# Turning first rows in single PSUM banks, long-filter rows by whole blocks, and the last hT turn later

## Chip, cores and metric

The kernel runs on one core of a Trainium2 chip. The metric is the device time of one execution in microseconds (us); smaller is better. TensorE is written PE in the profile, VectorE DVE, ScalarE ACT, GpSimd POOL and SyncE SP.

## The reference

A block of a network, forward and backward in one launch, in bf16, for 2048 rows of 1024 channels:

```python
xn = layernorm(A_q)                                  # rows of 1024
k_shift = 4-tap causal convolution of A_k along the rows
kv = k_shift * A_v
y = irfft(rfft(kv, 4096) * rfft(A_ssm_k, 4096))[:2048]   # long convolution, per channel
s = xn * (y + kv * A_ssm_D)
h = (xn @ B_w_gate) * (xn @ B_w_up)                  # 1024 -> 3584
out = A_q + s * silu(h @ B_w_down)                   # 3584 -> 1024
```

Returned are `out` and the gradients of all ten inputs but `B_x` for a given `grad_out`.

## The kernel before

A row tile is 128 rows; there are 16, numbered b. The work runs in stages, and PE carries matrix products in all of them:

- **Head, 0 to about 70 us.** `layer_norm` normalizes row tiles in chunks of 1, 1, 2, 4, 4 and 4 (`chunks`, `xs`): statistics on DVE (L584, L585), a root on ACT (L592), the normalizing itself on DVE (L603). Each tile is then turned (transposed) on PE in blocks of 128x128 into PSUM and copied by ACT into `XNT`, the stationary side of the products. Tiles 0 and 1 are turned in two halves of four blocks (L609, copied at L610), tiles 2 to 7 in one bank of eight (L620, copied at L621), and tiles 8 to 15 by `turn_late` (L571, copied at L631).
- **Gate and up products, 9 to about 505 us.** `gu_unit(sl, b0, n, ...)` multiplies n row tiles with a slab of 256 columns of both weights (L673, eight products of 512 columns for a row tile into one bank `psg` of `ps_gu`, which has two), copies to `gut` on ACT (L675) and stores it. A unit's element-wise product `hN` (called h, not the long filter) runs on DVE one unit later (`hn[0]`), and is turned to `hT` by `turn` or `turn_pair` through `defer` and `flush`, then stored from SP.
- **Forward long convolution, beside those products.** The generator `conv_forward` gives DVE work piece by piece. It is pumped by `tick`, which is called once for each row tile of a unit and lets the generator run up to a share of `F_TOTAL`; the yields are weights in us, less 0.95 of `pe_us`, an account of the PE work that it adds. Its PE parts are transforms (L234, L239, into `ps_cv`), inverse transforms (L455) and the turn of the long filter, `h_rows(ds)`, once for each of 8 groups of 128 channels: `hrow[:, c, u, r]` holds a filter's 2048 taps of a channel in a partition, and a block takes every eighth tap, so the columns of the stationary operand lie 8 elements apart. The result, scaled on ACT (L791), is `hx`.
- **Down product, 505 to 711 us**, `bm_first` and `late_mm` (L1032), in pairs of row tiles and 28 steps `fc`; a step of `bm_first` is a pair of products for each of two row tiles. After its first four steps `flush()` turns the last `hN`. Then the pools `ps_gu`, `fg` and `fw` go, and `ub` takes their room, into which the last weights `WD` and the next `ht` rows are loaded from SP.
- **Backward**, 700 us to the end.

Two forms of turning are in use. The plain one multiplies a block of 128 rows by the identity. `turn_halves` splits it into rows 0 to 63 and 64 to 127: two matmuls of 64 rows and 64 columns, with a result bank for each half; ACT's copy puts the halves together (`halves`).

PSUM has 8 banks. In the head `ps_tr` holds one tile `tr` of two banks (`tr_tile`, shared by `turn`, `turn_pair` and `h_rows`), `ps_gu` two banks, and `ps_st` one tile `turns` of four banks, out of which `next_bank` deals; after the head `ps_st` goes and `ps_cv` takes the four banks. Waits between engines are set by the framework from tiles, pools and the order of the program, which a scheduler rearranges; `tc.issue_after` and `keep_in_program_order` pin some of it.

Of the kernel before, what the change touches and what calls it, by code (L numbers as in the profile page):

```python
# [13 lines left out]
BF16 = mybir.dt.bfloat16  # L14
# [5 lines left out]
def build_kernel(  # L20
# [66 lines left out]
    def pool(name, bufs=1, side=None, space=None):  # L87
        kw = dict(name=name, bufs=bufs, reuse_waits="tile")
        if side:
            kw["side"] = side  # L90
        if space is not None:
            kw["space"] = space
        return tc.alloc_tile_pool(**kw)
# [425 lines left out]
    fg = pool("fg", 2, side="right")  # L519
    ps_tr = pool("ps_tr", 1, space=PSUM)  # L520
    ps_gu = pool("ps_gu", 2, space=PSUM)
    ps_st = pool("ps_st", 1, space=PSUM)
    turns = ps_st.tile([P, 4, 2, 4, P], BF16, name="tr")
    bank = [0]

    def next_bank():
        bank[0] += 1
        return turns[:, bank[0] % 4]

    busy = turns[:, 0].rearrange("p a b x -> p (a b x)").bitcast(F32).rearrange("p (a x) -> p a x", a=4)  # L530

    def keep_busy(n):
        for i in range(n):
# [40 lines left out]
    def halves(x):  # L574
        return x.rearrange("p b (h u) -> p h b u", h=2)

    def layer_norm(b0, n, x4):
        def small(name, dt=F32):
            return lns.tile([P, 4], dt, name=name)[:, 0:n]
        mv = lns.tile([P, 4, 2], F32, name="mv")[:, 0:n, :]  # L580
        for i in range(n):
            bst = lns.tile([P, 2, 6], F32, name="bst")
            for hh in range(2):
                V.bn_stats(out=bst[:, hh, :], in_=x4[:, i, hh * 512:(hh + 1) * 512])  # L584
            V.bn_aggr(out=mv[:, i, :], in_=bst[:])  # L585
        var_b = small("var_b", BF16)
        V.tensor_copy(var_b, mv[:, :, 1])
        vpe = small("vpe", BF16)
        V.tensor_scalar(vpe, var_b, EPS, None, op0=ADD)
        half_r = small("half_r")  # L590
        with tc.issue_after(act_copy[0].ins) if act_copy[0] is not None else nullcontext():
            root = nc.scalar.activation(half_r, vpe, ACT.Sqrt, scale=0.25)  # L592
        q0 = small("q0")
        rec = small("rec")
        V.reciprocal(rec, half_r)
        tt(q0, vpe, rec, MUL)
        sq_b = small("sq_b", BF16)
        V.scalar_tensor_tensor(sq_b, q0, 0.25, half_r, op0=MUL, op1=ADD)
        V.reciprocal(RSTD[:, b0:b0 + n], sq_b)
        for i in range(n):  # L600
            b = b0 + i
            q, qi = divmod(b, 4)
            last = V.tensor_scalar(x4[:, i, :], x4[:, i, :], mv[:, i, 0:1], RSTD[:, b:b + 1], op0=SUB, op1=MUL)  # L603
            if b < 2:
                for hh in range(2):
                    ps = next_bank()[:, 0]
                    for dc in range(4):
                        d0 = (4 * hh + dc) * P
                        tr_ln[0] = nc.tensor.transpose(ps[:, dc, :], x4[:, i, d0:d0 + P], ident[:])  # L609
                    act_copy[0] = nc.scalar.copy(out=XNT[0][:, 4 * hh:4 * hh + 4, b * P:b * P + P], in_=ps)  # L610
                if b == 0:
                    with tc.issue_after(tr_ln[0].ins):
                        keep_busy(10)
                continue
            if b0 >= 8:
                turn_rows.append((x4[:, i, :], q, qi))
                continue
            ps = next_bank().rearrange("p a b x -> p (a b) x")
            for dc in range(DC):
                tr_ln[0] = nc.tensor.transpose(ps[:, dc, :], x4[:, i, dc * P:(dc + 1) * P], ident[:])  # L620
            act_copy[0] = nc.scalar.copy(out=XNT[q][:, :, qi * P:(qi + 1) * P], in_=ps)  # L621
        c, r0 = divmod(b0, 8)
        return last, root, st(xnn[:, c, r0:r0 + n, :], x4[:, 0:n, :])

    def turn_late():
        ps = turns[:].rearrange("p (h j) i b x -> p h j i (b x)", h=2).rearrange("p h j i (a u) -> p h (j i) a u", u=64)
        for i, (x, q, qi) in enumerate(turn_rows):
            for dc in range(DC):
                tr_ln[0] = turn_halves(lambda hh: ps[:, hh, i, dc], x[:, dc * P:(dc + 1) * P])
        for i, (x, q, qi) in enumerate(turn_rows):  # L630
            act_copy[0] = nc.scalar.copy(out=halves(XNT[q][:, :, qi * P:(qi + 1) * P]), in_=ps[:, :, i])  # L631
        turn_rows.clear()

    nop = lambda: None
# [4 lines left out]
    def tr_tile():  # L639
        return ps_tr.tile([P, 2, 8, P], BF16, name="tr")  # L640
# [101 lines left out]
    def conv_forward():  # L742
# [33 lines left out]
            st(KSHd[dp], U[6][:].rearrange("p (b d) -> p b d", b=NB))  # L776
            yield 2.3

        def h_rows(ds):
            if ds == 8:  # L780
                return
            hrow = S_["h", ds]
            hx = S_["hx"] = cf.tile([P, NB, P], BF16, name="hx")
            pe_us[0] += 0.67
            ps = tr_tile()[:].rearrange("p h b x -> p h (b x)").rearrange("p h (b u) -> p h b u", u=64)
            with tc.issue_after(tr_ln[0].ins):
                turn_halves(lambda hh: ps[:, hh, 0], hrow[:, 0, :, 0])
            for b in range(1, 16):
                turn_halves(lambda hh: ps[:, hh, b], hrow[:, b // 8, :, b % 8])
            for c in range(2):  # L790
                nc.scalar.activation(halves(hx[:, 8 * c:8 * c + 8, :]), ps[:, :, 8 * c:8 * c + 8], ACT.Copy, scale=WSC)  # L791
            h_out.append(ds)
            if ds + 1 < 8:
                load_h(ds + 1)

        def kvs(ds):
            return S_["kvt", ds // 2][:, :, ds % 2 * P:(ds % 2 + 1) * P]
# [62 lines left out]
        yield from shift(0)  # L860
        PIN[0] = True
        yield 3.9
        h_rows(0)
        yield 0.1
        tl = turn_tables(ps_cv)
        sp = [half(0, S_["hx"], i, Dz[:, 0:P]) for i in range(2)]
        for ds in range(8):
            yield 0.5
            if ds % 2 == 1 and ds < 7:
                with tc.issue_after(S_["kst"].ins):  # L870
                    for c in range(2):
                        load_kv(ds // 2 + 1, c)
            D0 = Dz[:, ds * P:(ds + 1) * P]
            sph = []
            KX = cx.tile([P, 16, 256], BF16, name="KX")
            HX = cs.tile([P, 16, 256], BF16, name="HX", bufs=2)
            own_room = lambda X: X[:].rearrange("p a x -> p (a x)").bitcast(F32).rearrange("p (a x) -> p a x", a=8)[:, 0:4]
            eight = (ds, 1) in EIGHT
            if ds == 0:
                yield from transform(0, 1, sp, HX, own_room(KX), lambda i: sph.append(half(0, kvs(0), i)), nop)  # L880
            else:
                yield from transform(ds, 0, sp, KX, own_room(HX), lambda i: sph.append(half(ds, S_["hx"], i, D0)), nop)
                S_["kst"] = st(KFd[ds], KX[:])
            calls = []

            def behind():
                calls.append(0)
                if len(calls) % 2 == 0:
                    next(tl, None)
            room = cf.tile([P, 4, 256], F32, name="room", tag="hx")[:] if eight else None  # L890
            yield from transform(ds, int(ds > 0), sph, HX if ds else KX, room, nop1 if eight else lambda c: h_rows(ds + 1) if c == 0 else None,
                                 behind)
            if ds == 0:
                S_["kst"] = st(KFd[0], KX[:])
            if eight:
                h_rows(ds + 1)
            turned(HX, 1, 0, 1)
            yield 1.3
            if ds == 7:
                cf.release()  # L900
                S_["filters"] = False
            st(HFd[ds], HX[:])
            yield from product(KX, HX, KX, cs, False, 0)
            if ds % 2 == 1 and ds < 7:
                yield from shift(ds // 2 + 1)
            sp = []

            def ahead():
                if ds < 7:
                    sp.append(half(ds + 1, kvs(ds + 1), len(sp)))  # L910
            yield from (inv8 if ds in INV8 else inv_dft)(KX, HX, cs, ahead if ds % 2 == 0 else None, ahead)
            if ds % 2 == 1:
                ahead()
            S_["G", ds] = HX
            tl = tail(ds)
# [4 lines left out]
        cx.release()  # L920
        kst.release()

    F_TOTAL = 4 * SHIFT_W + 3.0 + 8 * (0.5 + FWD4_W + 1.3 + PROD_W + INV_W) + 10.0 - 0.95 * 8 * (4 * 1.75 + 0.67 + 4 * 0.9)
    F_TOTAL += len(EIGHT) * (FWD8_W - 9.6 + 0.95 * 1.75) - 2.0
    F_TOTAL += len(INV8) * (INV8_W - INV_W + 0.95 * 1.8)
    conv = conv_forward()
# [46 lines left out]
    st(RSTN[:], RSd.rearrange("(b p) -> p b", p=P))  # L973
    for p_ in (lnp, lns, tg, bsb):
        p_.release()
    ps_st.release()
    ps_cv = pool("ps_cv", 2, space=PSUM)
    pump, drain, step = make_pump(conv, F_TOTAL)
    cnt = [-5]
# [66 lines left out]
    cv_gone.append(True)  # L1046
    ps_bm = pool("ps_bm", 2, side="right", space=PSUM)
    pss = [ps_bm.tile([P, D], F32, name="psbm") for i in range(2)]
    with tc.issue_after(bm_first(range(4)).ins):
        flush()  # L1050
    for p_ in (ps_gu, fg, fw):
        p_.release()
# [11 lines left out]

    with tc.issue_after(wd_ld.ins):
        ht1 = load_ht1()
    fc_ = 4
    while conv_state["filters"]:
        bm_first([fc_])
        fc_ += 1  # L1070
# [735 lines left out]
```

## Time and profile before

| | us |
|---|---|
| median of 3 runs | 1915.76 (1915.6 to 1915.89) |
| profiled execution | 1915.97 |
| its span in the profile | 1914.2 |
| PE busy | 1895.2 (99%) |
| DVE busy | 1550.7 (81%) |
| ACT busy | 637.1 (33%) |

A line of the timeline gives the start in us, the length of the merged stretch, the engine, the source line, the operation, what it writes and reads, the shape, how many instructions are merged, and in brackets the idle time of the engine in front of it with what ended it. PEld is the loading of a stationary operand, which runs beside PE. Matmuls are pipelined: an instruction's own length is longer than the distance to the next start, so the time of a group is read from its start to the start of what follows.

### The profile page before, as it was taken

The numbers are of one execution on the slowest core, as the hardware profiler recorded it, in microseconds if no ns is written. First come the engines' busy times: TensorE is split into PE (matmuls) and PEld (weight loads), VectorE is DVE, ScalarE is ACT, GpSimd is POOL, SyncE is SP. The second block draws the span as 40 slices with busy tenths as digits, with TensorE's granted clock in tenths as the row PEclk, the third lists the DMA queues.
The fourth block names the chain that finished last, engine by engine and source line by source line (L and its number), as shares of the span: only waits on it lengthen the run. The fifth ranks groups of instructions, "written<-read, shape, count | busy, mean of one in ns | idle before, by whom it ended". The sixth has DMA issues, their size and how long they took to land.

```text
span 1914.2 us, 28265 instructions
## 1 busy us (share of the span) xinstructions
PE 1895.2 (99%) x11367; PEld 1014.8 (53%) x11507; DVE 1550.7 (81%) x1711; ACT 637.1 (33%) x927; POOL 334.8 (17%) x465
## 2 busy tenths in 40 slices
PE   8999999999999999999999999999999999999999
PEld 4555555545444456666666665664444444444444
DVE  7999999999988556887999999999995205678862
ACT  5765555546433233432222222222222102011122
POOL 5121212111113220001031221111212101112120
PEclk9999999999999999999999999999999999999999
DMA  8777866769769997677888698585887999889963
GB/s 285 269 251 232 257 224 207 234 233 296 248 228 311 313 306 230 208 239 229 275 264 264 221 266 267 181 286 177 227 245 173 221 203 180 182 176 195 194 162 124
DMA packets 425107, 444.35 MB, mean 232 GB/s; under 512 B 268400, under 2 KB 342796, under 8 KB 410512
## 3 DMA queue, kind: packets, MB, share of 16 engines
q1 hardware_dynamic: 367504, 239.03, 46.7%
q0 software_dynamic: 41152, 174.15, 29.3%
q10 hardware_dynamic: 16320, 29.36, 4.1%
q8 instruction: 90, 1.47, 0.3%
q14 instruction: 41, 0.34, 0.1%
HBM read 193.87 MB, written 189.84 MB: 200 GB/s over the span
## 4 chain that ended last, share of the span: by engine, by line
PE 96%; DVE 1%; issue 1%; ACT 1%; DMA 1%; SPq 0%; ACTq 0%; DVEq 0%
PE psb L1497 20%; PE psx L1642 20%; PE psg L673 19%; PE psb L1480 10%; PE psb L1580 9%; PE psbm L1032 9%; PE psF L234 3%; PE tr L571 1%; PE psI L455 1%; PE psY L1191 1%; PE psY L445 1%; PE psx L1580 1%; DMA U<-in_A_q_dram 1%; ACT U L631 0%; DVE bst L584 0%
## 5 line engine op out<-in xcount | busy, mean ns | idle before, releaser
L673 PE MATMUL psg<-wslab,U 128*128 128x512 bf16 x1728 | 399.0, 380 | 5.2 <-ACT gut L675 1.2
L1497 PE MATMUL psb<-U,U 128*128 128x512 bf16 x1792 | 397.1, 379 | 0.0
L1642 PE MATMUL psx<-U,dgut 128*128 128x512 bf16 x1505 | 331.0, 379 | 1.6
L1642 PEld LDWEIGHTS <-dgut 128*128 128x128 bf16 x1792 | 175.3, 98 | 211.4
L1497 PEld LDWEIGHTS <-U 128*128 128x128 bf16 x1792 | 175.2, 98 | 198.0
L673 PEld LDWEIGHTS <-U 128*128 128x128 bf16 x1792 | 172.4, 98 | 195.0 <-issue 3.5
L1480 PE MATMUL psb<-wdt,U 128*128 128x256 bf16 x1792 | 205.6, 273 | 0.0
L1480 PEld LDWEIGHTS <-U 128*128 128x128 bf16 x1792 | 175.3, 98 | 29.2
L212 DVE TENSOR_TENSOR W<-W 128x1024 f32<-128x1024 f32 (+1 forms) x189 | 186.5, 1003 | 4.1
L1580 PE MATMUL psb<-U,U 128*128 128x512 bf16 x797 | 176.1, 379 | 0.9
L1502 ACT CAST wb<-psb 128x512 bf16<-128x512 f32 x112 | 65.6, 586 | 315.4 <-PE psb L1497 313.4
L1247 DVE SCALAR_TENSOR_TENSOR dkp<-dkT,kT 128x1024 bf16<-128x1024 bf16 (+2 forms) x64 | 78.3, 1224 | 97.7 <-DMA dkT<-DKSHd 96.0
L1032 PE MATMUL psbm<-U,ht 128*128 128x512 bf16 x658 | 145.0, 379 | 0.7
L1580 PEld LDWEIGHTS <-U 128*128 128x128 bf16 x896 | 87.4, 98 | 104.3
L675 ACT CAST gut<-psg 128x512 bf16<-128x512 f32 x156 | 91.6, 589 | 117.0 <-PE psg L673 108.9
L1674 ACT ACTIVATE dx_t<-dxn 128x1024 bf16<-128x1024 f32 x15 | 15.9, 1057 | 323.1 <-DVE dxn L212 317.7
L1032 PEld LDWEIGHTS <-ht 128*128 128x128 bf16 x672 | 65.6, 98 | 78.2
L212 DVE TENSOR_TENSOR U<-U,dht 128x2048 bf16<-128x2048 bf16 x56 | 68.3, 1221 | 46.8 <-ACT dht L1482 46.7
L1482 ACT CAST dht<-psb 128x512 bf16<-128x512 f32 x112 | 65.6, 587 | 116.3 <-PE psb L1480 116.3
L66 POOL DMA_DIRECT2D Hd<-hN x54 | 37.3, 690 | 261.2 <-DVE hN L212 259.0
L1621 ACT CAST wbs<-psb 128x512 bf16<-128x512 f32 x51 | 29.9, 586 | 145.4 <-PE psb L1580 134.4
L212 DVE TENSOR_TENSOR W<-SP 128x1024 f32<-128x1024 f32 x64 | 74.2, 1218 | 1.6 <-ACT SP L295 1.1
(259 smaller groups left out, 2342.2 us busy)
## 6 DMA issues: line engine op xcount, KB each, us to landing
U<-GUd SPq DMA_DIRECT2D x28, 1024.0 KB, 8.9
DGd<-U SPq DMA_DIRECT2D x28, 1024.0 KB, 6.2
GUd<-gut ACTq DMA_DIRECT2D x39, 512.0 KB, 5.8
out_dram<-wb SPq DMA_DIRECT2D x112, 128.0 KB, 4.9
U<-Hd SPq DMA_DIRECT2D x14, 1024.0 KB, 6.7
Hd<-hN POOLq DMA_DIRECT2D x54, 256.0 KB, 5.0
HTd<-hT SPq DMA_DIRECT2D x24, 512.0 KB, 4.1
ht<-HTd SPq DMA_DIRECT2D x18, 512.0 KB, 7.6
```

Of the source, the lines that this page charges most:

```text
L212: pinned(V.tensor_tensor(o, a, b, op))
L234: mm = nc.tensor.matmul(ps[:, k].rearrange("p (c d) -> p c d", c=2), T[:, r, k, :], xr[:, r], start=(n == 0), stop=(n == len(rs) - 1 and ( ...
L673: gu_mm[0] = nc.tensor.matmul(ps[:], XNT[q][:, dc, qi * P:(qi + 1) * P], w[:, dc].rearrange("p a f -> p (a f)"), start=(dc == 0), stop=(dc ...
L675: nc.scalar.copy(out=gut[:, :, i], in_=ps[:].rearrange("p (a f) -> p a f", a=2))
L1032: mm = nc.tensor.matmul(ps[:, dh * 512:(dh + 1) * 512], ht(fc)[:, i * P:(i + 1) * P], WD[fc // 4][:, fc % 4, dh * 512:(dh + 1) * 512], sta ...
L1247: ins = V.scalar_tensor_tensor(prod[:].rearrange("p r d -> p (r d)")[:, lo:H], dkT[:, 0, lo:H], 1.0, kT[:, 0, 13 + m + lo:13 + m + H], op0 ...
L1480: nc.tensor.matmul(ps[:, x * SLW:(x + 1) * SLW], DBMT[2 * hf + g][:, dc, (b % 4) * P:(b % 4 + 1) * P], wdt[:, dc, :], start=(dc == 0), sto ...
L1482: nc.scalar.copy(out=dht[:, 2 * e:2 * e + 2].rearrange("p b f -> p (b f)"), in_=ps[:])
L1497: nc.tensor.matmul(ps[:], XN[b // 4][:, b % 4, dc * P:(dc + 1) * P], dgus[b // 8][:, :, b % 8], start=(b == 0), stop=(b == NB - 1))
L1502: nc.scalar.copy(out=wb[:, dc % 2].rearrange("p a f -> p (a f)"), in_=ps[:])
L1580: nc.tensor.matmul(ps, h[:, f, b, :], DBM[b // 4][:, b % 4, dh * 512:(dh + 1) * 512], start=(b == 0), stop=(b == NB - 1))
L1642: nc.tensor.matmul(ps[:, dh * 512:(dh + 1) * 512], t[n][:, f, i * P:(i + 1) * P], WGU[n][:, f, dh * 512:(dh + 1) * 512], start=(n == 0 and ...
```

## The change

- `ps_st` becomes a pool of four tiles of one bank each. `busy` and every turn of row tiles 0 to 7 take a tile of their own.
- In `turn_late` that pool is released and a pool of two tiles of two banks follows in the same four banks. Two row tiles are turned into one tile and copied, then the next two.
- `h_rows` turns the long filter plainly, in blocks of 128x128, in two calls of eight blocks (c = 0 and 1) into one bank each, with one ACT copy each. The calls stand where `transform` calls `ahead(0)` and `ahead(1)`, two pieces of DVE work apart (or before and after `turned` where the eight-point form is used). The weights in `pe_us` and `F_TOTAL` follow.
- The last `flush()` of `hT` comes after eight steps of `bm_first` in place of four.

The built program has 128 matmuls and 128 weight loads fewer on PE, and the same number of instructions on the other engines.

```diff
@@ -519,15 +519,9 @@
     fg = pool("fg", 2, side="right")
     ps_tr = pool("ps_tr", 1, space=PSUM)
     ps_gu = pool("ps_gu", 2, space=PSUM)
-    ps_st = pool("ps_st", 1, space=PSUM)
-    turns = ps_st.tile([P, 4, 2, 4, P], BF16, name="tr")
-    bank = [0]
-
-    def next_bank():
-        bank[0] += 1
-        return turns[:, bank[0] % 4]
-
-    busy = turns[:, 0].rearrange("p a b x -> p (a b x)").bitcast(F32).rearrange("p (a x) -> p a x", a=4)
+    ps_st = [pool("ps_st", 4, space=PSUM)]
+
+    busy = ps_st[0].tile([P, 4, P], F32, name="tr")
 
     def keep_busy(n):
         for i in range(n):
@@ -603,11 +597,11 @@
             last = V.tensor_scalar(x4[:, i, :], x4[:, i, :], mv[:, i, 0:1], RSTD[:, b:b + 1], op0=SUB, op1=MUL)
             if b < 2:
                 for hh in range(2):
-                    ps = next_bank()[:, 0]
+                    ps = ps_st[0].tile([P, 4, P], BF16, name="tr")
                     for dc in range(4):
                         d0 = (4 * hh + dc) * P
                         tr_ln[0] = nc.tensor.transpose(ps[:, dc, :], x4[:, i, d0:d0 + P], ident[:])
-                    act_copy[0] = nc.scalar.copy(out=XNT[0][:, 4 * hh:4 * hh + 4, b * P:b * P + P], in_=ps)
+                    act_copy[0] = nc.scalar.copy(out=XNT[0][:, 4 * hh:4 * hh + 4, b * P:b * P + P], in_=ps[:])
                 if b == 0:
                     with tc.issue_after(tr_ln[0].ins):
                         keep_busy(10)
@@ -615,20 +609,24 @@
             if b0 >= 8:
                 turn_rows.append((x4[:, i, :], q, qi))
                 continue
-            ps = next_bank().rearrange("p a b x -> p (a b) x")
+            ps = ps_st[0].tile([P, DC, P], BF16, name="tr")
             for dc in range(DC):
                 tr_ln[0] = nc.tensor.transpose(ps[:, dc, :], x4[:, i, dc * P:(dc + 1) * P], ident[:])
-            act_copy[0] = nc.scalar.copy(out=XNT[q][:, :, qi * P:(qi + 1) * P], in_=ps)
+            act_copy[0] = nc.scalar.copy(out=XNT[q][:, :, qi * P:(qi + 1) * P], in_=ps[:])
         c, r0 = divmod(b0, 8)
         return last, root, st(xnn[:, c, r0:r0 + n, :], x4[:, 0:n, :])
 
     def turn_late():
-        ps = turns[:].rearrange("p (h j) i b x -> p h j i (b x)", h=2).rearrange("p h j i (a u) -> p h (j i) a u", u=64)
-        for i, (x, q, qi) in enumerate(turn_rows):
-            for dc in range(DC):
-                tr_ln[0] = turn_halves(lambda hh: ps[:, hh, i, dc], x[:, dc * P:(dc + 1) * P])
-        for i, (x, q, qi) in enumerate(turn_rows):
-            act_copy[0] = nc.scalar.copy(out=halves(XNT[q][:, :, qi * P:(qi + 1) * P]), in_=ps[:, :, i])
+        if turn_rows and len(ps_st) == 1:
+            ps_st[0].release()
+            ps_st.append(pool("ps_s2", 2, space=PSUM))
+        for i in range(0, len(turn_rows), 2):
+            ps = ps_st[1].tile([P, 2, 2, DC, 64], BF16, name="tr2")
+            for j, (x, q, qi) in enumerate(turn_rows[i:i + 2]):
+                for dc in range(DC):
+                    tr_ln[0] = turn_halves(lambda hh: ps[:, hh, j, dc], x[:, dc * P:(dc + 1) * P])
+            for j, (x, q, qi) in enumerate(turn_rows[i:i + 2]):
+                act_copy[0] = nc.scalar.copy(out=halves(XNT[q][:, :, qi * P:(qi + 1) * P]), in_=ps[:, :, j])
         turn_rows.clear()
 
     nop = lambda: None
@@ -776,22 +774,23 @@
             st(KSHd[dp], U[6][:].rearrange("p (b d) -> p b d", b=NB))
             yield 2.3
 
-        def h_rows(ds):
+        def h_rows(ds, c):
             if ds == 8:
                 return
             hrow = S_["h", ds]
-            hx = S_["hx"] = cf.tile([P, NB, P], BF16, name="hx")
-            pe_us[0] += 0.67
-            ps = tr_tile()[:].rearrange("p h b x -> p h (b x)").rearrange("p h (b u) -> p h b u", u=64)
+            if c == 0:
+                S_["hx"] = cf.tile([P, NB, P], BF16, name="hx")
+            pe_us[0] += 0.47
+            ps = tr_tile()[:, 0]
             with tc.issue_after(tr_ln[0].ins):
-                turn_halves(lambda hh: ps[:, hh, 0], hrow[:, 0, :, 0])
-            for b in range(1, 16):
-                turn_halves(lambda hh: ps[:, hh, b], hrow[:, b // 8, :, b % 8])
-            for c in range(2):
-                nc.scalar.activation(halves(hx[:, 8 * c:8 * c + 8, :]), ps[:, :, 8 * c:8 * c + 8], ACT.Copy, scale=WSC)
-            h_out.append(ds)
-            if ds + 1 < 8:
-                load_h(ds + 1)
+                nc.tensor.transpose(ps[:, 0, :], hrow[:, c, :, 0], ident[:])
+            for r in range(1, 8):
+                nc.tensor.transpose(ps[:, r, :], hrow[:, c, :, r], ident[:])
+            nc.scalar.activation(S_["hx"][:, 8 * c:8 * c + 8, :], ps, ACT.Copy, scale=WSC)
+            if c == 1:
+                h_out.append(ds)
+                if ds + 1 < 8:
+                    load_h(ds + 1)
 
         def kvs(ds):
             return S_["kvt", ds // 2][:, :, ds % 2 * P:(ds % 2 + 1) * P]
@@ -860,7 +859,8 @@
         yield from shift(0)
         PIN[0] = True
         yield 3.9
-        h_rows(0)
+        h_rows(0, 0)
+        h_rows(0, 1)
         yield 0.1
         tl = turn_tables(ps_cv)
         sp = [half(0, S_["hx"], i, Dz[:, 0:P]) for i in range(2)]
@@ -888,14 +888,16 @@
                 if len(calls) % 2 == 0:
                     next(tl, None)
             room = cf.tile([P, 4, 256], F32, name="room", tag="hx")[:] if eight else None
-            yield from transform(ds, int(ds > 0), sph, HX if ds else KX, room, nop1 if eight else lambda c: h_rows(ds + 1) if c == 0 else None,
+            yield from transform(ds, int(ds > 0), sph, HX if ds else KX, room, nop1 if eight else lambda c: h_rows(ds + 1, c),
                                  behind)
             if ds == 0:
                 S_["kst"] = st(KFd[0], KX[:])
             if eight:
-                h_rows(ds + 1)
+                h_rows(ds + 1, 0)
             turned(HX, 1, 0, 1)
             yield 1.3
+            if eight:
+                h_rows(ds + 1, 1)
             if ds == 7:
                 cf.release()
                 S_["filters"] = False
@@ -920,7 +922,7 @@
         cx.release()
         kst.release()
 
-    F_TOTAL = 4 * SHIFT_W + 3.0 + 8 * (0.5 + FWD4_W + 1.3 + PROD_W + INV_W) + 10.0 - 0.95 * 8 * (4 * 1.75 + 0.67 + 4 * 0.9)
+    F_TOTAL = 4 * SHIFT_W + 3.0 + 8 * (0.5 + FWD4_W + 1.3 + PROD_W + INV_W) + 10.0 - 0.95 * 8 * (4 * 1.75 + 0.95 + 4 * 0.9)
     F_TOTAL += len(EIGHT) * (FWD8_W - 9.6 + 0.95 * 1.75) - 2.0
     F_TOTAL += len(INV8) * (INV8_W - INV_W + 0.95 * 1.8)
     conv = conv_forward()
@@ -973,7 +975,7 @@
     st(RSTN[:], RSd.rearrange("(b p) -> p b", p=P))
     for p_ in (lnp, lns, tg, bsb):
         p_.release()
-    ps_st.release()
+    ps_st[1].release()
     ps_cv = pool("ps_cv", 2, space=PSUM)
     pump, drain, step = make_pump(conv, F_TOTAL)
     cnt = [-5]
@@ -1046,7 +1048,7 @@
     cv_gone.append(True)
     ps_bm = pool("ps_bm", 2, side="right", space=PSUM)
     pss = [ps_bm.tile([P, D], F32, name="psbm") for i in range(2)]
-    with tc.issue_after(bm_first(range(4)).ins):
+    with tc.issue_after(bm_first(range(8)).ins):
         flush()
     for p_ in (ps_gu, fg, fw):
         p_.release()
@@ -1064,7 +1066,7 @@
 
     with tc.issue_after(wd_ld.ins):
         ht1 = load_ht1()
-    fc_ = 4
+    fc_ = 8
     while conv_state["filters"]:
         bm_first([fc_])
         fc_ += 1
```

## Prediction, made before the changed kernel ran

> **What bounds the kernel now.** I read four views in this order: the page, the windows of the first 70 us, the timeline around the turns (transpositions on TensorE), and the timeline of the head. The page first:
>
> ```profile
> span 1914.2 us, 28265 instructions
> PE 1895.2 (99%) x11367; PEld 1014.8 (53%) x11507; DVE 1550.7 (81%) x1711; ACT 637.1 (33%) x927; POOL 334.8 (17%) x465
> PE   8999999999999999999999999999999999999999
> PE 96%; DVE 1%; issue 1%; ACT 1%; DMA 1%; SPq 0%; ACTq 0%; DVEq 0%
> ```
>
> PE is busy for 99% of the span, and 96% of the chain that ended last lies on it; only the first slice (48 us) has room. So any TensorE time saved or added counts in full, a wait counts if PE waits, and nothing else counts. The windows (columns: length, then each engine's busy us, then the granted clock):
>
> ```profile
> 24.49:27.90 3.41, 0.90 (x11) 0.67 (x12) 2.90 (x12) 0.92 (x3) 0.00 (x0) 1.00 0.29 102
> 27.90:31.31 3.41, 3.19 (x16) 1.91 (x16) 3.41 (x9) 2.40 (x4) 2.54 (x4) 0.50 0.52 204
> 41.50:44.97 3.47, 2.26 (x15) 1.10 (x13) 3.37 (x10) 3.26 (x5) 3.21 (x5) 1.00 1.03 387
> ```
>
> PE was busy 0.90 of 3.41 us, and the next 3.41 us ran at half clock; with 2.26 of 3.47 busy the clock stayed. The turns, each read from its start to the start of what follows:
>
> ```profile
> 105.82 1.06 PE L192 MATMUL psT<-ident,TF 128*128 128x128 bf16 x16
> 106.81 1.16 PE L571 MATMUL tr<-ident,U 64*128 64x64 bf16 x32
> 107.90 1.47 PE L673 MATMUL psg<-wslab,U 128*128 128x512 bf16 x5
> ...
> 106.81 1.05 PEld L571 LDWEIGHTS <-U 64*128 64x128 bf16 x32
> ...
> 113.74 1.24 PE L673 MATMUL psg<-wslab,U 128*128 128x512 bf16 x5
> 114.91 0.64 PE L571 MATMUL tr<-ident,hN 64*128 64x64 bf16 x32
> 115.49 0.82 PE L673 MATMUL psg<-wslab,U 128*128 128x512 bf16 x2
> ```
>
> Sixteen plain turns of contiguous columns take 0.99 - 0.09 = 0.90 us, 0.056 per 128x128 block (the 0.09 is the price of entering the half-row form: five products at 0.216 end at 114.82, the halves start at 114.91). Thirty-two contiguous halves (hN) take 0.58 + 0.09 = 0.67. The 32 halves of a long-filter tile, whose columns lie 8 elements apart, take 1.09 + 0.09 to 1.10 + 0.10, so 1.19. Their loads set this: without the last load's own 0.17 us (the longest of this group by the view of line 571: 92/154/173 ns against 92/95/96 for hN), (1.05 - 0.17)/15 = 0.059 us for a pair of halves. The head:
>
> ```profile
> 18.63 1.88 DVE L584 BATCH_NORM_STATS2 bst<-U 128x6 f32<-128x512 bf16 x3 [2.00 <-DMA U<-in_A_q_dram]
> 20.43 1.04 DVE L212 TENSOR_TENSOR hN_s<-gut_s 128x256 bf16<-128x256 bf16 x1
> 27.00 0.62 PE L620 MATMUL tr<-ident,U 128*128 128x128 bf16 x8 [3.19 <-DVE U L603]
> 37.71 1.77 PE L571 MATMUL tr<-ident,U 64*128 64x64 bf16 x64
> 39.53 3.76 ACT L631 COPY U<-tr 128x1024 bf16<-128x1024 bf16 x4 [1.77 <-PE tr L571]
> 43.83 3.61 PE L673 MATMUL psg<-wslab,U 128*128 128x512 bf16 x16 [1.21 <-ACT gut L675]
> ```
>
> PE waits 3.19 us for rows 4 to 7, and 1.21 us for a psg bank that ACT empties only after four row copies; those started only once all 64 halves were done.
>
> **The change part by part.** The sum is made against the profiled execution, 1915.97 us (span 1914.2 and 1.8 around it), 0.2 above the median of 1915.76.
>
> *Long-filter turns, 8 of them.* Removed: 32 halves each, 1.19 us. Added: 16 plain turns of strided columns, a form that no row shows. Its nearest rows: plain contiguous, 0.056 per block, where the stream sets the pace; and the strided pair, 0.059 per block, where loading 2 x 64 rows side by side sets it. If 128 rows load as two halves side by side do and hide behind the stream, a turn costs 16 x 0.06 = 0.96, with nothing for changing the form. That is 8 x (0.96 - 1.19) = **-1.8 us**. Ends: 0.90 a turn (-2.3), and the two half loads one after the other, 0.119 per block, 1.90 a turn (+5.7). I take 0.96, since the strided pair moves the same elements.
> The Trainium skill (TensorEngine Tiling, section Theoretical Speedup) speaks against this edit: with a dimension of 64 or less, two tiles give up to 2x. By it, undoing the halves costs up to +1.19 a turn, +9.5 in all; the contiguous rows show 0.67 against 0.90, and the strided ones are bound by loads.
>
> *First rows, one bank each.* Before, all turns share one PSUM tile, and a turn into one bank waits for the copy out of another (0.67 us at 8.58, 0.24 at 12.18). This goes, but the next unit waits for the second slab anyway (0.30 us at 14.59), so it gives 0. The built order then differs twice. The multiply at 20.43 (1.04 us) stands ahead of the statistics of rows 4 to 7; its input is cast by 18.03, and DVE sits idle until 18.63 for the DMA, so the rows are ready about 1.0 earlier. And 57 instead of 53 products stand ahead of the wait for them: 4 x 0.216 = 0.9 of it is filled. Together **-1.9** (ends 0 and -2.6).
>
> *Late rows, two pairs of tiles.* Copies of rows 8 and 9 can start when their own halves are done, two DVE rows (2 x 0.48) earlier; of the wait of 1.21 I count **-0.7** (ends 0 and -1.2), and of the second one (0.34 us at 58.23) with its lead-in **-0.4** (0 to -0.5).
>
> *What is added on ACT and for the turning bank.* The long-filter turn now takes the single tr tile twice (a product group or more apart), each time until a 1.02 us copy is done; queued behind a turn that waits are all products, and the casts behind them. Before, with one take per turn, PE's waits in front of these turns are 0.0 to 0.1 us. The pump that paces the DVE work is shifted by the new weights too, and around 70 to 80 us ACT has the second copy between its casts and the spectra copies. Bounds: 0, and a whole copy each, 8.2. Most takes have 8 or more products (1.7 us) between, against a cast and a copy (1.6), so I take 0.2 for each of 8, **+1.6**.
>
> *Last hT turn, four pairs later.* In the built order 16 instead of 5 products stand between the first psI group and this turn, 11 x 0.216 = 2.4 us later. Behind it on SP's queue: its store (513.62), then the load of the last WD tile, allowed only after that store (519.41, landed at 524.83 by the DMA records), then eight ht loads. PE first reads that WD tile near 528.9: 4.1 of cover, 1.7 after. The first ht piece lands at 526.1, is wanted near 531.8, and keeps 3.3. Cost 0; if the load is slower by more than 1.7, PE waits for the rest, 1 to 2 us. The wait in front of the old turn (0.09 and 0.1) goes: **-0.1**.
>
> Sum: -1.8 - 1.9 - 0.7 - 0.4 + 1.6 - 0.1 = -3.3.
>
> *The clock.* With the rows ready near 25.9, PE is busy from there on: some 2.0 of the window 24.49 to 27.90, nearer to the 2.26 that kept the clock than to the 0.90 that lost it. At half clock PE lost at most 1.7 us of work, of which about 0.6 is not hidden behind DVE and ACT: **-0.6**. So -3.9, and 1915.97 - 3.9 = 1912.1; less the 0.2 to the median: **1911.8 us**.
>
> **The rivals.** What a measurement of this kernel can tell from no change is about 0.2%, 3.8 us: faster means under 1911.9, slower over 1919.6.
>
> A, the forecast: 1911.8, chance 0.42; its terms are good to about 1 us, and since it sits on the bound I count 0.28 of it as faster and 0.14 as the same.
>
> B, the clock falls all the same, because the window up to 27.90 holds almost only turns: without the 0.6 it is 1912.4. For it: four rows of turns and hardly a product. Against it: the halves and turns around 37.7 to 39.5 did not cost the clock, though they had products about them. The Trainium skill (TensorE: Matmul & The Clock Gate, Part 4: PE-mode transpose) says that turns do not count as busy in the way products do, which is this rival. Chance 0.20, of it 0.04 faster.
>
> D, the added waits do not come (no +1.6): 1910.2, chance 0.16. For it: hardly any wait at the tr tile before.
>
> E, the DVE convolution becomes the bound between 70 and 520 us, where its slices already show 9 tenths: what PE gains turns into waits for its operands, and only a tenth of the sum is left, 1915.4. Against it: PE waited for DVE under 2 us in that stretch. Chance 0.12, all the same.
>
> C, slower: a strided load of 128 rows takes what two half loads take in series. Place: the 8 long-filter turns. Price: +5.7 in place of -1.8, and with the other parts, -1.5 where the clock's 0.6 is left out, +4.2: 1919.9. It decides from about 0.09 us per block on; above that the turns eat the other gains. For it: no row shows the form. Against it: the two halves loaded together in 0.059. Chance 0.10. That the change does not do what it says is no separate case: the built order shows 256 turns of halves replaced by 128.
>
> **How the numbers follow.** Faster: 0.28 + 0.04 + 0.16 = 0.48. Same: 0.14 + 0.16 + 0.12 = 0.42. Slower: 0.10. The range leaves out C, a fourth of D and a third of E, 0.18 in all: 1910.0 to 1915.6.
>
> **What would show it.** In the changed profile: a long-filter turn of two groups of 8, each about 0.48 us to the next start (0.9 us or more would be C); rows 4 to 7 turned from about 25.9; a clock of 1.00 throughout 27.90 to 31.31 (0.50 would be B); the wait near 42 us for gut at half a microsecond or less; no wait of PE for a WD load near 526. Waits for tr copies or for DVE operands of 3 us or more between 70 and 520 us would make the forecast wrong, as would a stall at the WD tile.

## The result, and the profile after

The kernel after takes 1911.7 us in the median of 22 runs (1911.34 to 1916.43), the kernel before 1914.76 in 22 runs beside it (1913.28 to 1915.89): a ratio of 0.9986, 95% interval 0.998 to 0.9992. So it is faster by 2.7 us or 0.14%, less than the 0.2% from which on the prediction called a kernel faster. Its profiled execution took 1911.63 us. The three runs of before that the prediction started from, near 1915.76, are by their times of the longer of two kinds (experiment 1), and the prediction's mark of 1911.9 for faster was reckoned from them.

The page of the kernel after, the same rows as shown of before:

```profile
span 1909.9 us, 28150 instructions
...
PE 1899.4 (99%) x11379; PEld 1013.9 (53%) x11379; DVE 1549.7 (81%) x1711; ACT 636.8 (33%) x927; POOL 332.7 (17%) x465
...
PE   8999999999999999999999999999999999999999
...
PE 97%; DVE 1%; ACT 1%; DMA 0%; issue 0%; SPq 0%; ACTq 0%
```

The busy times have hardly moved, and PE still carries the chain. The 4.3 us between the two spans are all there when the first long-filter turn starts, at 62.99 us in place of 67.40; after it nothing is won. The windows of after:

```profile
24.49:27.90 3.41, 2.78 (x37) 2.20 (x37) 3.35 (x9) 2.69 (x5) 0.96 (x2) 1.00 0.41 135
27.90:31.31 3.41, 3.41 (x20) 1.60 (x19) 3.41 (x8) 3.03 (x6) 1.58 (x3) 1.00 0.96 352
```

Where PE had 0.90 us of work in the first window it has 2.78, and the clock in the second is 1.00 in place of 0.50. The timeline of after, PE, in the head:

```profile
8.93 1.67 PE L671 MATMUL psg<-wslab,U 128*128 128x512 bf16 x7 [0.80 <-DMA wslab<-in_B_w_gate_dram]
14.69 1.67 PE L671 MATMUL psg<-wslab,U 128*128 128x512 bf16 x7 [1.29 <-DMA wslab<-in_B_w_gate_dram]
25.34 1.99 PE L614 MATMUL tr<-ident,U 128*128 128x128 bf16 x32 [0.63 <-DVE U L597]
34.69 1.78 PE L565 MATMUL tr<-ident,U 64*128 64x64 bf16 x64 [0.72 <-DVE U L597]
36.40 2.33 PE L671 MATMUL psg<-wslab,U 128*128 128x512 bf16 x10
39.90 3.61 PE L671 MATMUL psg<-wslab,U 128*128 128x512 bf16 x16 [0.94 <-ACT gut L673]
```

Row 4 is turned at 25.34 in place of 27.00 and waits 0.63 in place of 3.19. But the first late rows now wait 0.72 for DVE, and the products behind them still 0.94 for a cast. A long-filter turn in after, PE:

```profile
61.70 1.46 PE L671 MATMUL psg<-wslab,U 128*128 128x512 bf16 x6
62.99 0.22 PE L786 MATMUL tr<-ident,U 128*128 128x128 bf16 x1
63.05 0.60 PE L788 MATMUL tr<-ident,U 128*128 128x128 bf16 x7
63.48 3.62 PE L671 MATMUL psg<-wslab,U 128*128 128x512 bf16 x16
```

Eight blocks take 63.48 - 62.99 = 0.49 us, 0.061 each. The six products before them are over at 61.70 + 6 x 0.216 = 63.00, so there is nothing to pay for entering the form; leaving it is inside the 0.49, which runs to the start of the next product. A tile of two such groups is 0.98, where the halves took 1.19.

### The profile page after: what moved, and what is told of

Read it like the earlier page. It is cut to its first block, busy times and chain, and to the rows that moved or that the text cites. A ratio compares the mean times of both kernels' runs of the same rounds, so it can differ in the third digit from the quotient of the medians.

```text
span 1909.9 us, 28150 instructions
## 1 busy us (share of the span) xinstructions
PE 1899.4 (99%) x11379; PEld 1013.9 (53%) x11379; DVE 1549.7 (81%) x1711; ACT 636.8 (33%) x927; POOL 332.7 (17%) x465
## 4 chain that ended last, share of the span: by engine, by line
PE 97%; DVE 1%; ACT 1%; DMA 0%; issue 0%; SPq 0%; ACTq 0%
PE psb L1499 20%; PE psx L1644 20%; PE psg L671 19%; PE psb L1482 10%; PE psbm L1034 10%; PE psb L1582 9%; PE psF L234 3%; PE psI L455 1%; PE tr L565 1%; PE psY L1193 1%; PE psY L445 1%; PE psx L1582 1%; DVE bst L578 0%; DMA wslab<-in_B_w_gate_dram 0%; PE tr L788 0%; DVE U L212 0%
```

## The experiments

The theory that these profiles suggest: the head and the clock give nearly all of the gain; the plain turns save what was forecast, but lose it again to waits. The main rival: the plain turns give a good part of the gain.

### 1. The clock in all runs

Each run's record has the mean granted clock, and it splits the runs cleanly: 0.999 where one stretch of 3.41 us ran at half clock, 1.000 where none did. Of 93 runs of before beside the experiments, 37 had it (mean 1915.74 us) and 56 had not (1913.99): the stretch costs 1.76 us, give or take 0.17. The profiled execution of before and the three runs first shown are of the longer kind. Of 33 runs of after, 32 have full clock, with a mean of 1911.94; the other took 1916.43, 4.5 more, and has no profile, so what made it longer is open. So from here on times are means of runs with full clock, and differences have 95% intervals made from the spread of these runs. Against 1913.99, after is 2.05 (+-0.18) faster.

Where the stretch falls is read from the windows of profiles with another start. They are set at its edges; the columns are length, then busy us of PE, PEld, DVE, ACT and POOL, then the clock. First the kernel of experiment 2 with plain turns, then that with single banks, then that with pairs of tiles:

```profile
22.71:26.13 3.42, 1.02 (x5) 0.28 (x3) 2.91 (x12) 0.68 (x2) 0.03 (x1) 1.00 0.60 198
26.13:29.54 3.41, 3.09 (x15) 1.81 (x16) 3.41 (x9) 1.75 (x3) 1.48 (x3) 0.50 0.35 132
```

```profile
8.08:11.49 3.41, 1.32 (x7) 0.64 (x8) 1.51 (x7) 0.31 (x2) 0.55 (x1) 1.00 0.97 297
11.49:14.90 3.41, 3.41 (x16) 1.62 (x15) 3.10 (x8) 1.56 (x3) 0.00 (x0) 0.50 1.14 365
```

```profile
22.17:25.58 3.41, 1.66 (x8) 0.57 (x6) 2.97 (x12) 0.68 (x2) 0.68 (x1) 1.00 0.79 271
25.58:29.00 3.42, 2.44 (x25) 1.66 (x26) 3.35 (x10) 1.78 (x5) 0.83 (x2) 1.00 0.23 78
```

In the recorded clock of every profile the edges lie on a grid of 3.413 us that starts at another point in each run (in before the clock rises at 7.43 and falls at 27.91, 6 x 3.413 later). A window of that grid with at most 1.32 us of PE work was followed by half clock (0.60, 0.91, 1.02 and 1.32 in four profiles); windows with 1.56 or more, in all thirteen profiles, were not. In the third kernel a wait of 2.73 us lies across an edge, and both windows keep enough. So it depends on where the grid falls in a run whether a wait of 2.7 to 3.2 us costs the clock. The Trainium skill (TensorE: Matmul & The Clock Gate, Part 1) describes such a free-running window of 3413 ns, and the traces agree. The rule of the Trainium skill in the same part (HAM oscillation), no pauses over about 3.4 us, is too mild here: waits of 2.3 to 3.2 us were enough.

### 2. Each part of the change alone, in the kernel before

**Plain turns alone.** `h_rows` as in the change, with its weights in `pe_us` and `F_TOTAL`:

```diff
-        def h_rows(ds):
+        def h_rows(ds, c):
...
-            turn_halves(lambda hh: ps[:, hh, b], hrow[:, b // 8, :, b % 8])
+            nc.tensor.transpose(ps[:, r, :], hrow[:, c, :, r], ident[:])
```

> The kernel before with the long-filter turns alone made plain, in two groups of 8 blocks, with their new place in the pump. Theory (the plain turns pay for themselves and no more): a turn falls from 1.19 to 0.98 us, 8 x 0.21 = 1.7 saved, and the waits that the trace after shows in front of them and of the convolution's other turns (0.16, 0.05, 0.36, 0.16, 0.17, 0.12, 0.12, 0.76, 0.12, 0.07, together 2.1) come back: +0.4, between 0 and +0.8. Rival 1 (most of those waits are not due to this edit): -1.7 to -1.0. Rival 2 (the prediction's terms as they stood, -1.8 + 1.6): -0.2. The head is that of before, so the wait of 3.2 us for row 4 and the half clock behind it should stay.

Measured: 1914.01 over 3 runs with full clock, +0.02 (+-0.32); 8 runs with the half stretch have a mean of 1915.73, against 1915.74. The plain turns give nothing by themselves that can be told from zero. Rival 1 falls; the theory's +0.4 and rival 2's -0.2 lie too close to tell apart with so few runs.

**Single banks alone:**

```diff
-    ps_st = pool("ps_st", 1, space=PSUM)
-    turns = ps_st.tile([P, 4, 2, 4, P], BF16, name="tr")
+    ps_st = [pool("ps_st", 4, space=PSUM)]
...
+            ps_st.append(pool("ps_s2", 1, space=PSUM))
+        turns = ps_st[1].tile([P, 4, 2, 4, P], BF16, name="tr2")
```

> The kernel before with the first eight rows alone turned into single banks of a pool; rows 8 to 15 are still turned all four into one tile of four banks. Theory: row 4 is turned 1.7 us earlier, four more products stand ahead of its wait, and the clock stays full behind it: the prediction's -1.9 and -0.6, so -2.5, between -2.0 and -3.2. Rival 1 (the slab transfers and the row copies that are late next eat the lead): -0.5 to -1.2. Rival 2 (the order is the same as before without the pairs of tiles): 0, with the wait of 3.2 us still there.

Measured: 1913.25, -0.74 (+-0.21); 1 of 11 runs has the half stretch. This comparison is at full clock on both sides, so of the theory's -2.5 only the -1.9 can show in it, and that is missed too. It is rival 1: the order did change and the clock stays, but part of the lead is lost on the way. The timeline of this kernel, PE:

```profile
26.67 1.99 PE L614 MATMUL tr<-ident,U 128*128 128x128 bf16 x32 [0.52 <-DVE U L597]
...
36.03 1.77 PE L565 MATMUL tr<-ident,U 64*128 64x64 bf16 x64 [0.72 <-DVE U L597]
...
42.15 1.02 PE L673 MATMUL psg<-wslab,U 128*128 128x512 bf16 x4 [1.85 <-ACT gut L675]
```

(Its profiled run is the one that lost the clock early, so its start times stand about 1.3 late.) Before and behind the late rows PE now waits 0.72 + 1.85 us, where the kernel before waits 1.21: the four row copies, which start only when all 64 halves are done, are the next thing that is late.

**Pairs of tiles alone:**

```diff
+        for i in range(0, len(turn_rows), 2):
+            ps = ps_st[1].tile([P, 2, 2, DC, 64], BF16, name="tr2")
```

> The kernel before with rows 8 to 11 and 12 to 15 alone turned in two tiles of two banks each. Theory: the row copies start while the second pair is turned, the wait of 1.21 us behind the first group falls to about 0.3 and that of 0.34 behind the second goes: the prediction's -0.7 and -0.4, so -1.1. Rival 1 (the trace after shows a wait of 0.94 for the gut cast at 38.96, so it only moved): -0.3 to -0.6, nearly all from the second group. Rival 2 (nothing of it reaches the end, since the units behind wait for something else): 0.

Measured: 1914.55 (3 runs), +0.56 (+-0.62); with the half stretch 1916.53 over 8 runs against 1915.74. So it is slower by some 0.7, which none of the three had expected. Timeline of this kernel, first PE at the first group, then ACT and PE at the second:

```profile
35.92 1.77 PE L571 MATMUL tr<-ident,U 64*128 64x64 bf16 x64 [0.16 <-DVE U L603]
37.63 2.98 PE L677 MATMUL psg<-wslab,U 128*128 128x512 bf16 x13
41.13 3.61 PE L677 MATMUL psg<-wslab,U 128*128 128x512 bf16 x16 [0.30 <-ACT gut L679]
```

```profile
50.78 1.28 ACT L181 ACT_TABLE_LOAD   x1
52.08 1.15 ACT L181 ACTIVATE TF<-m,negpi 128x1024 bf16<-128x1024 int32 x1
53.14 3.73 ACT L635 COPY U<-tr 128x1024 bf16<-128x1024 bf16 x4
56.74 0.62 ACT L679 CAST U<-psg 128x512 bf16<-128x512 f32 x1
```

```profile
57.41 2.97 PE L677 MATMUL psg<-wslab,U 128*128 128x512 bf16 x13 [2.22 <-ACT U L679]
```

The first group's wait fell from 1.21 to 0.30, but in this built order the second group's four copies and a table load stand ahead of a cast that empties a `psg` bank, and a wait of 0.34 became 2.22. In before and after one cast more stands between the table load and the copies (in after, the cast at 48.95, the copies from 49.61).

**Last turn of h alone:**

```diff
-    with tc.issue_after(bm_first(range(4)).ins):
+    with tc.issue_after(bm_first(range(8)).ins):
```

> The kernel before with the last turn of h alone put four pairs of products later. The turn at 509 us took 0.31 to enter and 0.57 after that in the trace after, against 0.40 and 0.80 before: -0.3. The prediction's term was -0.1. Rival (the transfers behind its store on SP's queue come late, PE waits for the last WD tile near 529): +0.5 to +2. Its head is that of before: if the wait of 3.2 us always brings the half clock, this profile shows it again at 27.9.

Measured: 1913.98 over 6 runs, -0.01 (+-0.68): too coarse to see 0.1 to 0.3, or to shut out the lower end of the rival. The trace decides against the rival: PE runs without a pause from 521 past 529, and no wait for a WD tile shows. Its profiled run has the half stretch behind the wait at 23.86, where the window before it has 0.60 us of PE work.

### 3. The head as a whole, and the rest on top of it

**Both changes of the head together,** the diffs of the single banks and of the pairs in one kernel.

> The kernel before with both changes of the head together (first eight rows in single banks, rows 8 to 15 in two tiles), nothing else. Against runs of before with the clock full (1913.9 mean): theory (the two parts need each other: the pairs alone put the second group's row copies ahead of a gut cast on ACT and cost 0.6, the first rows alone leave 1.85 us of wait behind the first group, together the casts stand as in the kernel after): -2.0, so 1911.9, nearly all of the whole change. Rival 1 (the parts add): -0.65 + 0.65 = 0, so 1913.9. Rival 2 (half of the whole change comes from the plain turns): -1.0, so 1912.9. The clock should stay full in all but one or two runs.

Measured: 1912.41, -1.58 (+-0.42; by the medians 1912.22 and 1914.08, -1.9), and full clock in all 11 runs. Rival 1 (the parts add) is out; the theory's -2.0 is at one edge of the interval and rival 2's -1.0 just outside the other, so the next run decides between these two. Alone the parts give -0.74 and about +0.6; together they give most of the change. Behind the first late group the two do add up. From the turn of row 8 to the product behind the cast it is 6.12 us in before (37.71 to 43.83) and with single banks (36.03 to 42.15), but 5.21 with pairs (35.92 to 41.13) and in after (34.69 to 39.90); and where the single banks are added to the pairs, row 8 is turned 1.23 earlier (34.69 against 35.92). What the pairs alone lose, they lose at the second group; with both changes the casts there stand as in after, and that wait does not come. Its three waits (0.86, 0.73, 0.94) are close to those of after (0.63, 0.72, 0.94).

**The kernel after with halves again,** in one call and with the old weights of the pump, so that the head and the last turn are what is left of the change:

```diff
-            pe_us[0] += 0.47
+            pe_us[0] += 0.67
...
-                nc.tensor.transpose(ps[:, r, :], hrow[:, c, :, r], ident[:])
+                turn_halves(lambda hh: ps[:, hh, b], hrow[:, b // 8, :, b % 8])
```

> The kernel after with the long-filter tiles turned in halves again, in one call, with the old weights of the pump. Theory (the plain turns pay for themselves and no more, as alone in the kernel before, +0.1): 1911.5 to 1912.0, against 1911.9, the mean of the kernel after. Rival (they save 1.7 in the kernel after, where the head is clear): 1913.5. A turn should take 1.19 us again, and the waits for the turning bank (0.115 to 0.17) and the one of 0.76 near 297 should go.

Measured: 1911.92. After is 0.02 (+-0.33) away from it. The plain turns are worth nothing in after either, so the main rival and rival 2 of the head's run are out, and the last turn is worth -0.49 (+-0.50) on top of the head. The halves take 1.1 us up to the next start again. The kernel after has waits of 0.16, 0.05, 0.36, 0.16, 0.17, 0.11, 0.12, 0.76, 0.07 and 0.12 us between 60 and 520 us, in all 2.1, counted from start to start; with the halves 0.3 of that is left.

### 4. Which waits eat the plain turns

**One call of 16 blocks:**

```diff
-            ps = tr_tile()[:, 0]
+            ps = tr_tile()[:]
...
-                nc.tensor.transpose(ps[:, r, :], hrow[:, c, :, r], ident[:])
+                nc.tensor.transpose(ps[:, b // 8, b % 8, :], hrow[:, b // 8, :, b % 8], ident[:])
```

> The kernel after with the 16 plain turns of a long-filter tile in one call, into both banks of the turning tile, at the place of the old halves. Theory (the waits belong to the split, since the turning tile is taken twice): most of the 2.1 us of added waits goes, the turns still take 0.98 or less: -1.0 to -1.7 against the kernel after, so 1910.2 to 1910.9. Rival 1 (the waits come from ACT's and DVE's order around the turn, not from the second take): 1911.5 to 1912. Rival 2 (a longer plain turn makes products wait): slower than 1912.2.

Measured: 1911.35, -0.59 (+-0.51) against after; less than the theory's -1.0 to -1.7, as the wait for DVE stays:

```profile
296.79 1.91 PE L234 MATMUL psF<-kv,TF 128*128 128x256 bf16 x16 [0.74 <-DVE kv L212]
```

The four waits between 70 and 80 us, 0.74 together, are gone. With two calls the second hx copy stands on ACT at 67.63, behind a cast, and the spectra copies start at 69.41; with one call both hx copies are done by 66.94 and the spectra copies start at 68.37. So the split cost some 0.6 of the 2.1, and the wait near 296 is not its doing.

**The old weights in the pump:**

```diff
-            pe_us[0] += 0.47
+            pe_us[0] += 0.335
-    F_TOTAL = ... - 0.95 * 8 * (4 * 1.75 + 0.95 + 4 * 0.9)
+    F_TOTAL = ... - 0.95 * 8 * (4 * 1.75 + 0.67 + 4 * 0.9)
```

> The kernel after with the old weights of the plain turns in the pump (0.67 a tile in place of 0.94), nothing else. Theory (the wait of 0.76 us for DVE near 297 follows from the shifted pump): it goes, so 1911.1. Rival (it follows from the order of the convolution's own work, whatever the weights): it stays, and the time is 1911.9 within 0.3.

Measured: 1911.27, -0.67 (+-0.27). The wait of 0.76 is gone. After first, then this kernel. The bracket says 0.59 because it counts from the end of the last product's own length; from start to start, 14 products from 293.69 on are over at 293.69 + 14 x 0.216 = 296.71, and the transform starts 0.76 later:

```profile
293.69 3.19 PE L671 MATMUL psg<-wslab,U 128*128 128x512 bf16 x14
297.47 1.91 PE L234 MATMUL psF<-kv,TF 128*128 128x256 bf16 x16 [0.59 <-DVE kv L212]
```

```profile
299.05 1.15 PE L234 MATMUL psF<-kv,TF 128*128 128x256 bf16 x9
```

In this built order more products stand in front of the transform (up to 299.05 without a pause), and the DVE product `kv` is done by then. The wait came from the account of PE's work, not from the turns.

**Both at once, the best version:**

> The kernel after with the 16 plain turns in one call into both banks, and the old weight of 0.67 for them in the pump. Theory (the two gains stand in different waits: the single call takes away most of the waits around the turns between 70 and 80 us, the old weight the wait near 296): against runs of the kernel after on the same chip, -0.7 - 0.6 = -1.3, so near 1910.4. Rival (both shift the same DVE order, and one takes the place of the other): 1911.0 to 1911.2. It would be the fastest of all.

Measured: 1910.66, -1.27 (+-0.38) against after, the sum of the two; against before a ratio of 0.9979, 95% interval 0.997 to 0.9988. It beats both kernels. Against the kernel with halves (1911.92) it is 1.26 faster, so most of the 1.7 that the plain turns have in store then arrives.

**After once more** on the same chip:

> The kernel after once more, unchanged, beside the two others on the same chip, and for the share of runs with the fallen clock. Every theory: 1911.7 within 0.3, the clock full in all but one or two runs.

Measured: 1912.07, full clock in all 11 runs; the best version is 1.40 (+-0.39) faster than these.

### 5. Is it the wait that costs the clock?

In the kernel before, 30 more products ahead of row 4's first turn; their results are not used.

```diff
+            if b == 4:
+                with tc.issue_after(last.ins):
+                    for k in range(30):
+                        fill = nc.tensor.matmul(busy..., XNT[0][:, 0, 0:P], slabs[0][:, 0]..., start=True, stop=True)
```

> The kernel before with 30 more products (of a slab, into a bank that the next turn overwrites; their results aren't used) ahead of row 4's first turn, so that 64 instead of 53 products stand ahead of the wait there. The extra work is 30 x 0.216 = 6.5 us, of which some 2.4 to 2.8 fill the wait. Theory (the wait of 2.7 to 3.2 us of idle TensorE is what lets the clock fall; it was there in 29 of 66 runs of before and in 2 of 77 of kernels without the wait): the wait shrinks to under 0.8, no run or at most one of 11 shows the fallen clock, and the time is 1914.0 + 6.5 - 2.6 = 1917.9, give or take 0.8 for the order behind it. Rival 1 (the fall has to do with something else of before's head, as turns in one tile of four banks): 4 to 8 of 11 runs still show it, and are 1.7 us longer than the others.

Measured: 1918.50 over 9 runs with full clock, inside the band expected. The timeline, PE:

```profile
19.68 6.63 PE L621 MATMUL tr<-wslab,U 128*128 128x512 bf16 x30
26.72 0.23 PE L624 MATMUL tr<-ident,U 128*128 128x128 bf16 x1 [0.40 <-DVE U L603]
```

One run took 1922.57 with a mean clock of 0.999, 4.1 longer than the others, and one took 2211.79 with 0.851, far outside everything else. So at most one of ten runs shows the fallen clock, where 4 in 10 of before do, and none shows the loss of 1.7. That is the theory's count: with the four banks still in one tile and only the wait filled, that kind of loss is gone. Ten runs make this likely, not certain: at a share of 0.40 as few as one would come up in about 5 of 100 such series. The kernels with the wait and without it say the same: 58 of 126 runs against 2 of 99.

## Why the prediction was right, and where two errors met

The forecast of 1911.8 against 1911.7 is better than its reasons, and that it is so close is luck. Its terms, in its own order:

- **Long-filter turns, -1.8:** right. 8 x (0.98 - 1.19) = -1.7. A block of 128 rows whose columns lie 8 apart is turned in 0.061 us, near the 0.056 of a contiguous one and far from the 0.119 that the prediction gave for two loads in series, so rival C is out. The up to 2x of the Trainium skill (TensorEngine Tiling (Array Packing), Theoretical Speedup) does not show for this operand: the halves are the slower form.
- **First rows, -1.9:** right up to the late rows. Row 4 is turned at 25.34, against 26.56 in the pairs-alone kernel, whose head is before's with full clock, and 4 more products are done by then: -1.2 - 0.9. That the ACT waits of the first turns would go to the slab was right as well: the slab waits are 0.80 and 1.29, where the plain-turns-alone kernel has 0.55 and 0.49.
- **First late group, -0.7: this step failed.** The prediction took the wait behind the late rows as fixed and subtracted from it. That the pairs bring the copies some 0.9 forward was right (5.21 in place of 6.12). But against the pairs-alone kernel PE comes to the late rows 1.8 earlier (33.97 in place of 35.76, the turn's start less its wait) and row 8 is ready only 1.2 earlier (34.69 in place of 35.92), so PE waits for DVE. And 3 of the 4 products that were won ahead of row 4 are missing behind the late rows, 10 in place of 13, which is 0.65 more of waiting for the cast. So 0.72 + 0.94 stand where 1.21 stood, +0.45 in place of -0.7; the wait for the cast alone should have been half a microsecond or less. The second group's -0.4 came (0.34 is gone). The head by its waits: -2.1 + 0.45 - 0.34 = -2.0; by the runs -1.58 (+-0.42); forecast -3.0.
- **Added waits, +1.6:** the right size in the wrong places, which is luck. 2.1, less the 0.3 that the halves have too, is 1.8. Only 0.5 of it stands at the turning bank, where the prediction put all; 0.74 comes from ACT's order between 70 and 80 us, which the prediction named without a price, and 0.76 from the pump. Turns and waits: -0.2 forecast, 0.0 measured. Rival D is out.
- **Last turn, -0.1:** the wait in front of it, 0.185 in the trace of the head alone, is in after the 0.096 that entering the halves costs elsewhere too: -0.09, and no stall at the WD tile. By the runs it is -0.49 (+-0.50), which does not contradict this.
- **The clock, -0.6: this step failed too.** That it would hold was right. Of the 1.7 us of lost PE work the prediction let DVE and ACT hide 1.1; they hide nothing that shows, the price is 1.76 (+-0.17). And the 0.2 to the median was a step between runs of the longer kind, when 6 in 10 runs of before have no such stretch.

So from a run of before with the stretch, 1915.74 - 1.76 - 1.58 - 0.49 + 0.02 = 1911.93. The head with the last turn gave 2.1 where 3.1 was forecast, the turns gave nothing where 0.2 was forecast, the clock gave 1.76 where 0.6 was forecast: 1.2 too much and 1.2 too little, and the two met. Rival B, that the clock falls because the window holds almost only turns, failed on its own ground. The kernel with halves again had the first of these windows on its grid, the kernel after the second:

```profile
24.62:28.04 3.42, 2.50 (x36) 2.10 (x36) 3.35 (x10) 2.58 (x4) 0.86 (x2) 1.00 0.37 118
33.58:37.00 3.42, 2.55 (x69) 1.46 (x68) 3.31 (x9) 1.80 (x4) 1.84 (x4) 1.00 0.81 207
```

Of the 2.50 us, 2.0 are 32 whole turns and 0.5 are products, and of the 2.55, 1.8 are 64 turns of halves; no later window in these two profiles ran below 1.00, where 1.32 us of PE work had lost the clock. The rule of the Trainium skill that turns do not count as busy (TensorE: Matmul & The Clock Gate, Part 4) is not borne out here. Rival E is out as well: 1.26 of the 1.7 that the plain turns gain arrive as soon as the call and the pump are mended.

## What to carry to other kernels

When a wait ends, ask who comes early to the next meeting point and who does not. Each of the two head changes alone gave little or cost time, and both together gave the gain. Work moved ahead of one wait is missing behind the next. Before a difference under 0.2% is read, split the runs by their mean granted clock, since one drawn stretch at half clock was worth nearly as much as the whole change. An account that paces other work belongs to the change: here two numbers in it cost 0.7 us, a third of what the kernel gained at equal clock.

## What the runs showed of the hardware that was not expected

- In 13 profiles the clock changes on a grid of 3.413 us whose start differs from run to run; windows with up to 1.32 us of PE work lost it, windows from 1.56 on kept it, and a lost one costs 1.76 us where PE is the bound.
- Turns kept the clock: windows of the grid with 2.50 and 2.55 us of PE work, of which 2.0 and 1.8 were turns, were followed by full clock.
- A stationary block with its columns 8 elements apart costs 0.061 us to turn, against 0.056 for a contiguous one, and changing from products to the plain form costs nothing (62.99 in after), while the half-row form costs about 0.1 on entering (0.096 at 509.03 in after) and about 0.1 on leaving (0.107 more before the product at 509.60 than from half to half).
